# Seven half products in place of eight: the out product of blocks 1 to 8 by Strassen's scheme

## The chip, the core and the metric

The kernel runs on one core of one Trainium2 chip. The metric is the device time of one execution in microseconds (us); most executions of a kernel lie within 1% of each other. The engines are called as the profile calls them: PE is TensorE (matmuls; PEld is its weight load), DVE is VectorE, ACT is ScalarE, POOL is GpSimd, SP is the engine whose queue issues all DMA here.

## The reference

```python
# q, k, v: (8, 8, 576, 64); attention inside chunks of 64 tokens
scores = matmul(q_c, k_c.transpose(...)) / sqrt(64)
attn = softmax(scores)
x = matmul(attn, v_c)  -> tokens x 512      # 4608 x 512
a = x @ w_a                                 # 512 x 1536
b = x @ w_b
out = (a * b) @ w_out                       # 1536 x 512, float32
```

## The kernel before

The 4608 tokens are taken as 9 blocks of 512 (block 0 to 8). Each block has 12 ff tiles of 128; for each tile there are 8 matmuls of 512 columns, then ACT copies `b` out of PSUM and DVE multiplies it with `a` into `ab[ft]`. After the 12 tiles comes the out product, four groups of 128 tokens, 12 matmuls each.

```python
F = [pp.tile([128, 512], FP32, name=f"F{i}") for i in range(4)]   # a ring of four PSUM banks

def ffn_close(K, ft, us, banks):
    bT = ring("b", bsb)
    nc.scalar.copy(out=bT[:, 0:n], in_=banks[0][:, 0:n])
    nc.vector.tensor_tensor(out=ab[ft][...], in0=banks[1][:, 0:n], in1=bT[:, 0:n], op=MULT)

def out_products(tg, ft, o):
    nc.tensor.matmul(o, ab[ft][:, tg * 128:(tg + 1) * 128], wo[ft // 2][:, ft % 2, :],
                     start=(ft == 0), stop=(ft == NFT - 1))

def out_close(K, tg, o):
    t = ring("o", osb)
    nc.vector.tensor_copy(out=t, in_=o)
    # ... one or two stores to out from the SP queue
```

Attention runs in between, in units of 256 tokens. A unit goes through a chain of its own: loads of q, k, v (SP queue), casts to bf16 (GpSimd), a DMA transpose of q and k (SP queue), then the scores on PE. The order in which the program names these steps is the order in each engine's queue:

```python
for K in range(2, NBLK):
    for s in range(NFT + 4):
        step()                                   # a late normalise (DVE) or exp (ACT)
        if s < NFT: ffn(K, s)
        else:       outs(K, (s - NFT,))
        for s0, u in ((2, 2 * K + 3), (10, 2 * K + 4)):
            if s == s0 and u - 1 < NU: slot(u - 1, u if u < NU else None)  # sums, values, scores on PE
            if s == s0 + 1: cast_unit(u + 1)     # three casts on GpSimd, each waits for its DMA
            if s == s0 + 3:
                turn_unit(u + 1)                 # DMA transpose
                load_unit(u + 2)
```

Block 1 has the same parts, but its ff tiles are done in two halves of 256 tokens, because its second half's attention is not ready at first.

The softmax here doesn't subtract the row's maximum and nothing guards it: scores larger than these inputs give would overflow.

## Time and profile before

| | before |
|---|---|
| time, median | 328.55 us (3 runs, 328.37 to 329.36) |
| PE busy | 313.8 of 326.9 us |
| DVE, ACT, POOL busy | 130, 124, 76 us |
| one block, 3 to 6 | 33.1 us |
| its out product | 10.36 us: 48 matmuls of 512 columns, 216 ns each |

The profile's page gives in part 1 the busy time of each engine and its share of the span, and in part 4 the shares of the chain of work that ended last:

```profile
PE 313.8 (96%) x2698; PEld 155.4 (48%) x2698; DVE 129.9 (40%) x206; ACT 123.9 (38%) x200; POOL 76.3 (23%) x95
...
PE 80%; DMA 11%; SPq 3%; DVE 2%; ACT 2%; issue 1%; POOL 0%; DVEq 0%
```

The chain of waits of the kernel before, in order of time (start us, length us, what). L384 are the ff matmuls, L406 those of the out product, L237, L253 and L220 the attention's:

```profile
57.68 0.87 PE F L384 x8
...
116.48 10.36 PE F L406 x48
126.84 5.18 PE F L384 x24
...
132.93 13.92 PE F L384 x64
...
147.76 1.83 PE F L384 x8
149.59 10.36 PE F L406 x48
```

Two out products start 149.59 - 116.48 = 33.1 us apart, and the chain names nothing but PE in between. So in these blocks only fewer PE cycles can save time. The first line, of block 1, tells the price of a matmul of 256 columns: 0.87 us for 8, 109 ns each, half of 216.

In block 1 a second chain runs nearly as fast as PE. The timeline of the kernel before (start us, length us, engine, line, operation, tile, and in brackets the idle time before it and its releaser), for unit 5:

```profile
70.23 1.04 POOL L158 CAST qkb<-f 128x1024 bf16<-128x1024 f32 x1 [3.51 <-DMA f<-in_q_dram]
72.38 1.04 POOL L158 CAST qkb<-f 128x1024 bf16<-128x1024 f32 x1 [1.11 <-DMA f<-in_k_dram]
73.45 1.59 SPq L202 DMA_TRANSPOSE qkT<-qkb  x1
...
78.27 0.47 PE L220 MATMUL PS<-qkT 64*64 64x64 bf16 x32
```

The casts wait for DMA, the transpose for the casts, and the scores (L220) start at 78.27. A transpose takes 3.9 us in the median from issue to landing.

### The profile page before, as it was taken

What the parts mean: (1) busy time and instruction counts of PE and PEld (TensorE: products, weight loads), DVE (VectorE), ACT (ScalarE), POOL (GpSimd) and SP (SyncE); (2) the same over time, 40 slices, a digit from 0 to 9 for tenths busy, and PEclk for the clock granted to TensorE, in tenths of its full rate; (3) what the DMA queues carried; (4) which work ended last, traced back from release to release, by engine and by line L of the source; (5) the groups of instructions that cost most, each with busy time, mean ns of one, the idle gap of its engine ahead of it and who ended that gap; (6) DMA issues with size and microseconds to landing.
All of it is one profiled execution on the core that took longest, in us unless ns stands there. A gap on an engine that the chain in (4) does not pass through costs nothing.

```text
span 326.9 us, 6552 instructions
## 1 busy us (share of the span) xinstructions
PE 313.8 (96%) x2698; PEld 155.4 (48%) x2698; DVE 129.9 (40%) x206; ACT 123.9 (38%) x200; POOL 76.3 (23%) x95
## 2 busy tenths in 40 slices
PE   7599998999999999999999999999999999999995
PEld 3334444877444444444444444444444444444442
DVE  2434433444244443534253434443444353423431
ACT  3533314666326331634163416340635063303310
POOL 2556953232232231230123003210330000000000
PEclk9879999999999999999999999999999999999999
DMA  7999997999997959960996099808970600030002
GB/s 220 235 321 384 402 254 237 214 242 214 206 262 171 217 131 243 232 136 35 225 249 138 20 162 266 201 32 202 253 159 13 181 4 0 8 116 7 0 34 96
DMA packets 145693, 54.95 MB, mean 168 GB/s; under 512 B 126208, under 2 KB 139520, under 8 KB 145664
## 3 DMA queue, kind: packets, MB, share of 16 engines
q1 hardware_dynamic: 145664, 54.54, 65.6%
q8 instruction: 21, 0.34, 0.4%
q14 instruction: 8, 0.07, 0.1%
HBM read 37.75 MB, written 9.44 MB: 144 GB/s over the span
## 4 chain that ended last, share of the span: by engine, by line
PE 80%; DMA 11%; SPq 3%; DVE 2%; ACT 2%; issue 1%; POOL 0%; DVEq 0%
PE F L384 49%; PE F L406 26%; DMA wst<-in_moe_w_a_dram 5%; DMA f<-in_k_dram 3%; SPq L140 2%; PE F L237 2%; PE PS L220 2%; DMA f<-in_q_dram 1%; SPq L133 1%; PE PA L253 1%; DMA out_dram<-osb 1%; ACT inv L267 1%; DVE osb L416 1%; ACT lns L263 1%; DVE xT L272 0%
## 5 line engine op out<-in xcount | busy, mean ns | idle before, releaser
L395 ACT CAST bsb<-F 128x512 bf16<-128x512 f32 (+1 forms) x120 | 64.8, 541 | 154.1 <-PE F L384 153.9
L384 PE MATMUL F<-xT,wb 128*128 128x512 bf16 (+1 forms) x480 | 114.4, 360 | 2.6 <-DVE xT L272 1.3
L384 PE MATMUL F<-xT,wa 128*128 128x512 bf16 (+1 forms) x480 | 114.0, 359 | 1.0 <-DVE ab L396 0.4
L396 DVE TENSOR_TENSOR ab<-F,bsb 128x512 bf16<-128x512 f32 (+1 forms) x120 | 76.2, 637 | 90.7 <-PE F L384 84.6
L406 PE MATMUL F<-wo,ab 128*128 128x512 bf16 x432 | 95.4, 379 | 0.0
L384 PEld LDWEIGHTS <-wa 128*128 128x128 bf16 x480 | 46.9, 98 | 48.8 <-issue 2.1
L384 PEld LDWEIGHTS <-wb 128*128 128x128 bf16 x480 | 45.6, 98 | 47.8 <-issue 4.0
L158 POOL CAST qkb<-f 128x1024 bf16<-128x1024 f32 (+1 forms) x37 | 36.0, 973 | 134.7 <-DMA f<-in_q_dram 108.2
L406 PEld LDWEIGHTS <-ab 128*128 128x128 bf16 x432 | 42.0, 98 | 50.1
L416 DVE COPY osb<-F 128x512 f32<-128x512 f32 x36 | 24.8, 691 | 56.3 <-PE F L406 53.1
L272 DVE TENSOR_TENSOR xT<-PA,inv 128x512 bf16<-128x512 f32 x32 | 21.9, 686 | 30.1 <-ACT inv L267 30.1
L158 POOL CAST vb<-f 128x1024 bf16<-128x1024 f32 (+2 forms) x22 | 19.5, 887 | 25.8 <-DMA f<-in_v_dram 20.8
L263 ACT ACTIVATE lns<-F 128x512 f32<-128x512 f32 x32 | 17.4, 594 | 15.3 <-PE F L237 15.3
L231 ACT ACTIVATE E<-PS 128x1024 bf16<-128x1024 f32 (+1 forms) x20 | 18.8, 941 | 7.2 <-PE PS L326 4.5
L267 ACT ACTIVATE inv<-lns 128x1024 f32<-128x1024 f32 x16 | 16.9, 1057 | 0.5
L158 POOL CAST wa<-wst 128x512 bf16<-128x512 f32 x12 | 7.4, 616 | 3.2 <-DMA wst<-in_moe_w_a_dram 3.1
L158 POOL CAST wb<-wst 128x512 bf16<-128x512 f32 x12 | 7.4, 616 | 3.2 <-DMA wst<-in_moe_w_b_dram 3.0
L253 PEld LDWEIGHTS <-vb 64*64 64x64 bf16 x512 | 7.2, 109 | 1.6
L220 PE MATMUL PS<-qkT 64*64 64x64 bf16 x512 | 7.8, 202 | 0.0
L156 ACT COPY qkT<-F 128x512 bf16<-128x512 bf16 (+1 forms) x5 | 3.8, 757 | 10.2 <-PE F L180 6.9
L253 PE MATMUL PA<-E,vb 64*64 64x64 bf16 x512 | 7.2, 192 | 0.0
L158 DVE COPY qkT<-F 128x512 bf16<-128x512 bf16 x9 | 5.3, 601 | 4.6 <-PE F L303 4.2
(31 smaller groups left out, 54.7 us busy)
## 6 DMA issues: line engine op xcount, KB each, us to landing
out_dram<-osb SPq DMA_DIRECT2D x32, 256.0 KB, 2.2
f<-in_q_dram SPq DMA_DIRECT2D x28, 256.0 KB, 3.8
f<-in_k_dram SPq DMA_DIRECT2D x28, 256.0 KB, 4.3
f<-in_v_dram SPq DMA_DIRECT2D x28, 256.0 KB, 4.6
wst<-in_moe_w_out_dram SPq DMA_DIRECT2D x6, 512.0 KB, 9.2
wst<-in_moe_w_b_dram SPq DMA_DIRECT2D x5, 512.0 KB, 8.8
wst<-in_moe_w_a_dram SPq DMA_DIRECT2D x5, 512.0 KB, 8.4
f<-in_v_dram SPq DMA_DIRECT2D x16, 128.0 KB, 4.2
```

The source lines that it names most:

```text
L158: eng.tensor_copy(out=out, in_=in_)
L220: nc.tensor.matmul(o, t[j * 64:j * 64 + 64, 8 + 4 * g + m, cl * 64:cl * 64 + 64], qt, start=True, stop=True,)
L231: nc.scalar.activation(out=e[:, :, s], in_=PS[:, :, s], func=AF.Exp, scale=scale)
L253: nc.tensor.matmul(PA[j * 64:j * 64 + 64, cl, c:c + 64], vb[u % 3][cl * 64:cl * 64 + 64, g * 512 + h * 64:g * 512 + h * 64 + 64], e[cl * 6 ...
L263: nc.scalar.activation(out=lns[:, cl, :], in_=SU[cl], func=AF.Ln)
L267: nc.scalar.activation(out=inv[u % 2][:, s, :], in_=lns[:, s, :], func=AF.Exp, scale=-1.0)
L272: nc.vector.tensor_tensor(out=x.rearrange("p m (g c t) -> p c g m t", g=2, c=2)[:, cl], in0=PA[:, cl, :].rearrange(shape, g=2, m=4), in1=i ...
L384: nc.tensor.matmul(bank[:, 0:n], w[ft // 2][ft % 2][:, kt, :], x[:, kt, us[0] * 256:us[0] * 256 + n], start=(kt == 0), stop=(kt == NKT - 1),)
L395: nc.scalar.copy(out=bT[:, 0:n], in_=banks[0][:, 0:n])
L396: nc.vector.tensor_tensor(out=ab[ft][:, us[0] * 256:us[0] * 256 + n], in0=banks[1][:, 0:n], in1=bT[:, 0:n], op=MULT)
L406: nc.tensor.matmul(o, ab[ft][:, tg * 128:(tg + 1) * 128], wo[ft // 2][:, ft % 2, :], start=(ft == 0), stop=(ft == NFT - 1),)
L416: nc.vector.tensor_copy(out=t, in_=o)
```

## The change

With token halves h, ff tiles taken as pairs (f = 0 the even, 1 the odd tile), and column halves c, the out product of a block is a 2 by 2 product of matrices. Strassen's scheme does it in seven half products where the plain way needs eight, at the price of sums ahead of the products and after them. Here that is, per block, 84 matmuls of 256 columns (7 products, 6 pairs, 2 groups of 128 tokens) for 48 of 512 columns: 1/8 less PE work. The sums of `w_out` are made once, on GpSimd, in block 1; those of `ab` by DVE, three instructions for each pair; the products are put together by ACT, DVE and GpSimd.

```diff
+    def sum_wo(i, eng):                       # GpSimd, 6 pairs, once
+        b = staged["o", i].rearrange("p (x c) -> p x c", x=4)
+        y = wsum[:, i]
+        eng.tensor_tensor(out=y[:, 0:2], in0=b[:, 0:4:2], in1=b[:, 1:4:2], op=ADD)
+        eng.tensor_tensor(out=y[:, 2], in0=b[:, 1], in1=b[:, 3], op=SUB)
+        eng.tensor_tensor(out=y[:, 3], in0=b[:, 2], in1=b[:, 0], op=SUB)
+        eng.tensor_tensor(out=y[:, 4], in0=b[:, 0], in1=b[:, 3], op=ADD)
+
+    def sum_ab(i):                            # DVE, 6 pairs in every block
+        a = ab2[i].rearrange("p f (h t) -> p (f h) t", h=2)
+        y = asum[:, i]
+        nc.vector.tensor_tensor(out=y[:, 0:2], in0=a[:, 0:2], in1=a[:, 2:4], op=ADD)
+        nc.vector.tensor_tensor(out=y[:, 2:4], in0=a[:, 1:3], in1=a[:, 0:4:3], op=SUB)
+        nc.vector.tensor_tensor(out=y[:, 4], in0=a[:, 0], in1=a[:, 3], op=ADD)
+
+    def outs_fast(K, t):                      # t: which 128 tokens of each half
+        ...                                   # product(): 6 matmuls of 256 columns into the next bank of F
+        A.copy(out=m3, in_=product(of_ab(0, 0), of_wsum(2)))
+        A.copy(out=m4, in_=product(of_ab(1, 1), of_wsum(3)))
+        add(G, w, m3, m4)
+        add(V, w, product(of_asum(4), of_wsum(4)), w)
+        add(V, oa[:, HF:DM], product(of_asum(0), of_wo(1, 1)), m3)
+        add(G, y1, w, oa[:, HF:DM], SUB)
+        add(V, ob[:, 0:HF], product(of_asum(1), of_wo(0, 0)), m4)
+        add(G, y2, w, ob[:, 0:HF], SUB)
+        add(V, oa[:, 0:HF], product(of_asum(3), of_wsum(1)), y1)
+        store(K, t, oa)
+        add(V, ob[:, HF:DM], product(of_asum(2), of_wsum(0)), y2)
+        store(K, 2 + t, ob)
 ... (block 0 to block 1)
         cast_unit(3, (2,))
+        for i in range(3):
+            sum_wo(i, G)
 ... (block 1, first half)
             if ft == 3:
                 cast_unit(4)
+                for i in range(3, 6):
+                    sum_wo(i, G)
 ... (block 1, second half; the later blocks likewise)
             ffn(1, ft, (1,))
+            if ft % 2:
+                sum_ab(ft // 2)
 ...
-        for tg in range(4):
+        for t in range(2):
             step()
-            outs(1, (tg,))
+            outs_fast(1, t)
 ... (blocks 2 to 8)
-            for s in range(NFT + 4):
+            for s in range(NFT + 2):
```

The weight sums and the `ab` sums lie in the space of the weight staging buffers. The ring `osb` grows from three buffers to four.

More of the change, by code (lines that the diff above doesn't have):

```diff
@@ L27 @@
     MULT = mybir.AluOpType.mult
+    ADD = mybir.AluOpType.add
+    SUB = mybir.AluOpType.subtract
     B, H, S, D = q.shape
@@ L75 @@
     xT = [buf(f"xT_{i}", [128, NKT, BLK], BF16) for i in range(3)]
-    ab = [buf(f"ab_{i}", [128, BLK], BF16) for i in range(NFT)]
     bsb = [buf(f"bsb_{i}", [128, BLK], BF16) for i in range(3)]
-    osb = [buf(f"osb_{i}", [128, DM], FP32) for i in range(3)]
+    osb = [buf(f"osb_{i}", [128, DM], FP32) for i in range(4)]
     NP = NFT // 2
+    ab2 = [buf(f"ab_{i}", [128, 2, BLK], BF16) for i in range(NP)]
+    ab = [ab2[i // 2][:, i % 2, :] for i in range(NFT)]
     wa = [[buf(f"wa_{i}_{h}", [128, NKT, 128], BF16) for h in range(2)] for i in range(NP)]
@@ L84 @@
     NWS = 10
-    wst = [buf(f"wst_{i}", [128, 1024], FP32) for i in range(NWS)]
+    wsta = buf("wst", [128, NWS * 1024], FP32)
+    wst = [wsta[:, i * 1024:(i + 1) * 1024] for i in range(NWS)]
+    HF = DM // 2
+    wsum = wsta[:, 0:4 * 1024].bitcast(BF16)[:, 0:NP * 5 * HF]
+    wsum = wsum.rearrange("p (i n c) -> p i n c", i=NP, n=5)
+    asum = wsta[:, 4 * 1024:8 * 1024].bitcast(BF16)[:, 0:NP * 5 * HF]
+    asum = asum.rearrange("p (i n t) -> p i n t", i=NP, n=5)
+    part = buf("part", [128, 2, 5, HF], FP32)
     state = {"f": 0, "b": 0, "o": 0, "w": 0}
@@ L416, in out_close, with store @@
         nc.vector.tensor_copy(out=t, in_=o)
+        store(K, tg, t)
+    def store(K, tg, t):
         for p, n, b, s0 in runs(2 * K + tg // 2, tg % 2):
@@ L427, in outs, with product, of_ab, of_wo @@
             out_close(K, tg, o[k])
+    def sum_wo(i, eng):
[12 more added lines that the diff above has]
+    def outs_fast(K, t):
+        c = t * 128
+        m3, m4, w, y1, y2 = [part[:, t, n, :] for n in range(5)]
+        oa, ob = ring("o", osb), ring("o", osb)
+        V, A, G = nc.vector, nc.scalar, nc.gpsimd
+        def product(a, b):
+            o = nextF()[:, 0:HF]
+            for i in range(NP):
+                nc.tensor.matmul(
+                    o, a(i)[:, c:c + 128], b(i), start=(i == 0), stop=(i == NP - 1)
+                )
+            return o
+        def of_ab(f, h):
+            return lambda i: ab2[i][:, f, h * HF:(h + 1) * HF]
+        def of_wo(f, h):
+            return lambda i: wo[i][:, f, h * HF:(h + 1) * HF]
+        def of_asum(n):
+            return lambda i: asum[:, i, n]
+        def of_wsum(n):
+            return lambda i: wsum[:, i, n]
+        def add(eng, out, in0, in1, op=ADD):
+            eng.tensor_tensor(out=out, in0=in0, in1=in1, op=op)
+        A.copy(out=m3, in_=product(of_ab(0, 0), of_wsum(2)))
[10 more added lines that the diff above has]
+        store(K, 2 + t, ob)
     def fill(n):
@@ L432, in fill @@
             nc.tensor.matmul(PA[:, 0, :], zero[:, 0:128], zero, start=True, stop=True)
+    staged = {}
     with tc.manual_schedule():
@@ L450 @@
         load_half_v(0, nc.sync)
-        staged = {}
         def queue_half(i, h, ns):
@@ L670 @@
                 load_unit(7)
-        for tg in range(4):
+        for t in range(2):
             step()
-            outs(1, (tg,))
-            if tg == 1:
+            outs_fast(1, t)
+            if t == 0:
                 slot(5, 6)
                 cast_unit(7)
-            if tg == 2:
+            if t == 1:
                 turn_unit(7)
@@ L684 @@
                     ffn(K, s)
+                    if s % 2:
+                        sum_ab(s // 2)
                 else:
-                    outs(K, (s - NFT,))
+                    outs_fast(K, s - NFT)
                 for s0, u in ((2, 2 * K + 3), (10, 2 * K + 4)):
```

## The prediction

> **What bounds it now.** TensorE: busy 313.8 of 326.9 us (busy table), and the chain of waits is 80% PE. From 96 us on the slices by stage show PE fully busy: a block takes 33.1 us, of it 10.36 us out product (48 matmuls of 512 columns, 216 ns each, chain), 20.7 us ffn and about 1.9 us attention. Before 120 us there is a second chain: load, GpSimd cast, DMA transpose, next load (DMA share 0.93). In block 1 the DMA transposes of units 5 and 6 land about 0.9 and 0.2 us before their scores start (73.45 + 3.9 against 78.27; 83.72 + 3.9 against 87.7).
>
> **What the change does on PE.** 84 matmuls of 256 columns replace 48 of 512 in each of 8 blocks. 256-column matmuls already run in block 1 at 109 ns each (chain: 0.875 us for 8), with their weight loads hidden. So 9.2 us for 10.36: 1.15 us a block, 9 us in all, if nothing waits.
>
> **What it adds.**
> - DVE: 18 bf16 sums a block. Two tensor inputs in SBUF and 16-bit: the Trainium skill ("VectorE: DVE Perf Modes", perf-mode tier table) gives two elements a cycle; with the fixed 160 ns of this trace's casts that is an estimated 1.15 us per ff pair, 7 us a block. Plus ten 256-wide PSUM adds of 0.42 us for four 0.69 us copies. DVE goes from 13.5 to about 22 us of 33: not the bound in blocks 2 to 8, but in block 1's second half (256 wide) it needs 2.0 us a pair against 1.75 of PE.
> - The third half product needs the last pair's sums: about 2.4 us after the last ffn matmul, wanted at 1.8. PE waits about 0.5 us a block. The net gain of a steady block is then about 0.5 us.
> - GpSimd: 24 weight sums in block 1. No such op is in the trace; casts are 190 ns + 0.83 ns an element (1042 ns for 1024, 402 for 256). The skill ("GPSIMD Engine Reference", section 3) puts a two-input op at 2.6 cycles an element; my estimate is 0.7 us for 256 and 1.25 for 512, 3.3 us a pair, 20 us in all, in two lumps ahead of the casts of units 4 and 5. The transpose of unit 5 moves from 73.5 to about 80 us: PE waits about 5 to 6 us at its scores.
> - The block sums on GpSimd stand behind the casts of the next unit, which wait for DMA. In blocks 1 and 2 those casts end about 5 us or more after the out product starts, so DVE's first combine keeps its PSUM bank and, with 4 banks, the seventh product waits: about 4 us in block 1, 2.5 in block 2. From block 3 on the casts end about in time.
> - All four stores of a block now precede the next transpose and loads on the SP queue: 4 to 5 us later, just in time.
>
> **Sum.** Blocks 1 and 2: +12 us. Blocks 3 to 8: -3. Predicted 337.5 us, 8 in 10 between 330 and 345. Faster by over 2%: 0.05; within 2%: 0.30; slower by over 2%: 0.65.
>
> **What would show it.** Out-product matmuls at 109 ns; PE idle before scores about 78 us released by the transpose; PE idle inside the out products of blocks 1 and 2 released by a DVE add that waited for GpSimd; GpSimd adds of 0.7 us; a block of 32.5 us after block 3; a short PE wait in the third product.
>
> **What would make it wrong.** GpSimd adds near 0.83 ns an element (about 332 us); casts that come early enough; DVE sums at one element a cycle or blocked by GpSimd (later, above 340); late transposes in every block.

## The result

| | before | after |
|---|---|---|
| median | 328.96 us (4 runs) | 339.19 us (4 runs, 337.29 to 340.07) |
| ratio | | 1.0295, 95% interval 1.0237 to 1.0354: slower |
| profiled span | 326.9 us | 338.3 us |
| PE busy | 313.8 us | 309.2 us |
| DVE busy | 129.9 us | 196.0 us |
| POOL busy | 76.3 us | 131.6 us |

A ratio is the mean time of one kernel's runs over that of the other's of the same rounds, so it is not quite the ratio of the medians.

```profile
PE 309.2 (91%) x2955; PEld 184.5 (55%) x2986; DVE 196.0 (58%) x398; ACT 135.8 (40%) x232; POOL 131.6 (39%) x167
...
PE 56%; DMA 16%; SPq 8%; POOL 8%; DVE 4%; issue 4%; ACT 3%; POOLq 0%; DVEq 0%
```

These are parts 1 and 4 of the page after. PE works less, but its share of the chain fell from 80% to 56%; POOL, which had 0% of it, has 8%, and the shares of DMA and of the SP queue have grown. Where this happens is told by the times at which each block's first ff matmul starts in the PE timelines (all in us, read from the two traces; the last row is worked out):

| | block 1 | block 2 | block 3 | 4 | 5 | 6 | 7 | 8 to the end |
|---|---|---|---|---|---|---|---|---|
| before | 38.13 | 33.37 | 33.12 | 33.12 | 33.11 | 33.12 | 32.82 | 34.94 |
| after | 50.65 | 34.63 | 32.50 | 32.43 | 33.20 | 32.43 | 32.44 | 33.95 |
| difference | +12.52 | +1.26 | -0.62 | -0.69 | +0.09 | -0.69 | -0.38 | -0.99 |

Blocks 3 to 8 win 3.3 us together. Block 1 loses 12.5 us and block 2 1.3 us. The remaining 0.9 us of the 11.4 lies before block 1 (it starts at 55.17 and 56.07 us); over all runs below that start varies from 53.7 to 56.6 us with the clock that PE is granted in its first 25 us (0.72 before, 0.57 after, between 12 and 24 us). Of the change that span holds only the first few weight sums on GpSimd (from 53.02 us), and the out product of block 0 takes 14.50 us here as in the last two runs below, which have no sum there. So I compare block by block where I can.

A steady block after, in its chain of waits (L397 are ff matmuls, L475 those of the half products, L462 to L464 the three `ab` sums of a pair):

```profile
158.84 2.75 PE F L397 x12
161.59 0.40 PE F L250 x4
...
164.18 0.22 DVE xT L285
...
164.79 0.69 DVE ab L409
...
165.50 0.42 DVE wst L462
165.93 0.34 DVE wst L463
166.26 0.21 DVE wst L464
...
166.52 7.49 PE F L475 x67
```

The chain leaves PE at the end of the block's ff tiles and goes over the last `ab` product and its three sums: the third half product reads the sum that DVE makes last (L464). From the start of the out product (164.17) to the next ff matmul (173.85) it is 9.68 us.

Block 1 after, in the timeline (L453 are weight sums on GpSimd, L171 casts, L215 the transpose, L233 the scores, L493 the combining adds):

```profile
67.52 1.27 POOL L453 TENSOR_TENSOR wst<-wst 128x512 bf16<-128x512 f32 x1
...
72.76 0.95 DVE L462 TENSOR_TENSOR wst<-ab 128x512 bf16<-128x512 bf16 x1
73.64 0.94 DVE L463 TENSOR_TENSOR wst<-ab 128x512 bf16<-128x512 bf16 x1
74.50 1.34 DVE L464 TENSOR_TENSOR wst<-ab 128x256 bf16<-128x256 bf16 x1
...
76.23 0.60 PE L397 MATMUL F<-xT,wa 128*128 128x256 bf16 x4 [1.43 <-DVE ab L409]
...
77.92 2.27 POOL L171 CAST qkb<-f 128x1024 bf16<-128x1024 f32 x2
...
79.69 0.60 PE L397 MATMUL F<-xT,wa 128*128 128x256 bf16 x4 [1.55 <-DVE ab L409]
80.23 1.60 SPq L215 DMA_TRANSPOSE qkT<-qkb  x1
82.24 0.60 PE L397 MATMUL F<-xT,wa 128*128 128x256 bf16 x4 [0.65 <-DVE ab L409]
84.03 0.45 PE L233 MATMUL PS<-qkT 64*64 64x64 bf16 x32 [0.58 <-DMA qkT<-qkb]
...
101.61 1.04 POOL L171 CAST vb<-f 128x1024 bf16<-128x1024 f32 x1 [0.84 <-DMA f<-in_v_dram]
102.61 0.72 POOL L493 TENSOR_TENSOR part<-part 128x256 f32<-128x256 f32 x1
103.37 0.42 DVE L493 TENSOR_TENSOR part<-F,part 128x256 f32<-128x256 f32 x1 [5.64 <-POOL part L493]
103.84 1.17 PE L475 MATMUL F<-wst 128*128 128x256 bf16 x6 [4.45 <-DVE part L493]
...
106.72 0.58 PE L397 MATMUL F<-xT,wb 128*128 128x512 bf16 x1 [1.71 <-DVE xT L285]
```

Three things are to be seen. First, unit 5's transpose is issued at 80.23 for 73.45, because its casts stand in GpSimd's queue behind the weight sums; the scores come at 84.03 for 78.27. Second, before that PE already waits 1.43, 1.55 and 0.65 us for `ab` products of DVE, whose sums take two to five times as long here as in the steady block (L464: 1.34 us for 0.28). Third, the last cast of unit 7 waits for its load until 101.61, and the combining add of GpSimd stands behind it; DVE waits for that add, keeps its PSUM bank, and the seventh product waits 4.45 us for the bank. In the first group of the same block that wait is 1.62 us.

The windows view of the kernel after, with the busy time of each engine in us, then PE's granted clock, DMA share and GB/s, shows an after-effect of the 4.45 us:

```profile
98.00:104.00 6.00, 1.55 (x15) 1.23 (x14) 0.63 (x2) 0.00 (x0) 2.77 (x3) 1.00 0.62 176
104.00:108.00 4.00, 2.07 (x9) 1.04 (x9) 1.90 (x5) 0.00 (x0) 1.41 (x2) 0.52 0.41 137
108.00:112.00 4.00, 4.00 (x13) 1.50 (x12) 0.69 (x1) 1.91 (x3) 0.00 (x0) 0.63 0.96 217
```

The clock drops to 0.52 and 0.63 after the pause. The Trainium skill ("TensorE: Matmul & The Clock Gate", the table "Why this matters for your kernels") warns of PE-idle gaps over about 3 us; this trace agrees. The runs below put the limit somewhat lower: after the first 25 us, PE waits of 2.49, 2.83, 2.87, 3.80, 4.37 and 7.57 us were each followed by a clock near 0.50 for some us, and none of 2.18 us or less at full clock was. What this fall costs can be estimated from the lines above: 2.07 us of PE work at 0.52 and 4.00 us at 0.63 are 2.5 us more than at full clock. About 2 us of that lie in block 2, which took 34.63 us for the 32.43 of a steady block, though PE had no wait over 0.22 us in it.

### The profile page after: what moved, and what is told of

It is laid out like the page before. It is cut to its first block, busy times and chain, and to the rows that moved or that the text cites. A ratio compares the mean times of both kernels' runs of the same rounds, so it can differ in the third digit from the quotient of the medians.

```text
span 338.3 us, 7477 instructions
## 1 busy us (share of the span) xinstructions
PE 309.2 (91%) x2955; PEld 184.5 (55%) x2986; DVE 196.0 (58%) x398; ACT 135.8 (40%) x232; POOL 131.6 (39%) x167
## 4 chain that ended last, share of the span: by engine, by line
PE 56%; DMA 16%; SPq 8%; POOL 8%; DVE 4%; issue 4%; ACT 3%; POOLq 0%; DVEq 0%
PE F L397 39%; PE F L475 15%; DMA f<-in_k_dram 6%; DMA wst<-in_moe_w_a_dram 4%; DMA f<-in_v_dram 3%; SPq L123 3%; SPq L153 2%; ACT inv L280 2%; DMA f<-in_q_dram 2%; POOL qkb L171 1%; SPq L146 1%; POOL wst L453 1%; DVE ab L409 1%; PE F L250 1%; DMA qkT<-qkb 1%
## 5 line engine op out<-in xcount | busy, mean ns | idle before, releaser
L397 PE MATMUL F<-xT,wa 128*128 128x512 bf16 (+1 forms) x478 | 114.4, 361 | 4.7 <-DVE ab L409 3.8
L397 PE MATMUL F<-xT,wb 128*128 128x512 bf16 (+1 forms) x454 | 112.9, 361 | 5.4 <-DVE xT L285 3.0
L397 PEld LDWEIGHTS <-wa 128*128 128x128 bf16 x480 | 47.1, 98 | 52.3 <-issue 6.9
L397 PEld LDWEIGHTS <-wb 128*128 128x128 bf16 x480 | 46.0, 99 | 48.9 <-issue 7.3
L171 POOL CAST qkb<-f 128x1024 bf16<-128x1024 f32 (+1 forms) x37 | 36.4, 986 | 90.7 <-DMA f<-in_q_dram 64.5
L475 PEld LDWEIGHTS <-wst 128*128 128x128 bf16 x480 | 46.4, 98 | 14.8 <-issue 6.4
L475 PE MATMUL F<-wst 128*128 128x256 bf16 x288 | 38.7, 275 | 7.1 <-DVE part L493 6.1
L493 POOL TENSOR_TENSOR part<-part 128x256 f32<-128x256 f32 x16 | 11.6, 728 | 69.2 <-ACT part L496 69.2
L493 DVE TENSOR_TENSOR osb<-F,part 128x256 f32<-128x256 f32 x64 | 26.9, 423 | 11.3 <-POOL part L493 9.4
L171 POOL CAST vb<-f 128x1024 bf16<-128x1024 f32 (+2 forms) x22 | 20.1, 914 | 21.1 <-DMA f<-in_v_dram 17.0
L493 POOL TENSOR_TENSOR part<-part,osb 128x256 f32<-128x256 f32 x32 | 22.6, 728 | 14.5 <-DVE osb L493 14.5
L475 PE MATMUL F<-wst,ab 128*128 128x256 bf16 x192 | 24.7, 273 | 0.9 <-DVE ab L409 0.9
L462 DVE TENSOR_TENSOR wst<-ab 128x512 bf16<-128x512 bf16 x48 | 24.2, 504 | 1.8
L475 PE MATMUL F<-wo,wst 128*128 128x256 bf16 x192 | 23.6, 273 | 0.0
L463 DVE TENSOR_TENSOR wst<-ab 128x512 bf16<-128x512 bf16 x48 | 22.8, 474 | 0.0
L475 PEld LDWEIGHTS <-ab 128*128 128x128 bf16 x192 | 18.7, 98 | 6.2 <-DVE ab L409 1.9
L493 DVE TENSOR_TENSOR part<-F,part 128x256 f32<-128x256 f32 x16 | 6.8, 425 | 24.8 <-PE F L475 14.6
```

The source lines that it names most:

```text
L171: eng.tensor_copy(out=out, in_=in_)
L397: nc.tensor.matmul(bank[:, 0:n], w[ft // 2][ft % 2][:, kt, :], x[:, kt, us[0] * 256:us[0] * 256 + n], start=(kt == 0), stop=(kt == NKT - 1),)
L462: nc.vector.tensor_tensor(out=y[:, 0:2], in0=a[:, 0:2], in1=a[:, 2:4], op=ADD)
L463: nc.vector.tensor_tensor(out=y[:, 2:4], in0=a[:, 1:3], in1=a[:, 0:4:3], op=SUB)
L475: nc.tensor.matmul(o, a(i)[:, c:c + 128], b(i), start=(i == 0), stop=(i == NP - 1))
L493: eng.tensor_tensor(out=out, in0=in0, in1=in1, op=op)
```

## The experiments

Two theories were held against each other. **Theory Q**: the time is lost in the queue of GpSimd, where the weight sums stand ahead of casts that a transpose waits for, and the combining adds behind casts that a load is waited for. **Theory D**: it is lost on DVE, which carries 66 us more work, and whose sums PE waits for. Block lengths are read from the profiled run.

### Weight sums left out

```diff
-        for i in range(3):
-            sum_wo(i, G)
 ...
-                for i in range(3, 6):
-                    sum_wo(i, G)
 ... (block 0, before cast_pairs(2, 0, G))
+        for i in range(6):
+            V.memset(wsta[:, 640 * i:640 * (i + 1)], 0.0)
```

Expected:

> Wrong result on purpose: the 24 weight sums on GpSimd in block 1 are not done; the same store is filled with zeros by DVE in block 0, where DVE waits for DMA anyway. Theory Q (the queue of GpSimd: weight sums stand ahead of the casts of units 4 and 5, whose transposes and following loads come late): the transpose of unit 5 is issued near 74 us again instead of 80.2, and the time falls by 5 to 8 us, to 331 to 334; what stays is the wait of the out product of block 1 for the combining adds behind the casts of units 6 and 7. Theory D (the sums on DVE are what PE waits for: DVE is busy 196 us against 130): they all stay, so less than 3 us is won, 336 to 339.

Measured: 333.41 us median (330.57 to 335.03), ratio to before 1.0111 (1.0051 to 1.0171); the result is wrong. Block 1 takes 44.46 us for 50.65. The transpose of unit 5 is issued at 74.93. Of the long waits only those for the seventh product (2.87 us) and for the late normalise at the start of block 2 (2.06 us) are left:

```profile
98.14 0.81 PE L475 MATMUL F<-wst 128*128 128x256 bf16 x6 [2.87 <-DVE part L493]
101.01 0.59 PE L397 MATMUL F<-xT,wb 128*128 128x512 bf16 x1 [2.06 <-DVE xT L285]
```

So the 24 weight sums cost 6.2 us of block 1's 12.5. The zeros in their place did not make PE faster by themselves: a steady block takes 32.43 us here as in the changed kernel. Theory D's range is missed.

### Combining adds on DVE

```diff
-        V, A, G = nc.vector, nc.scalar, nc.gpsimd
+        V, A, G = nc.vector, nc.scalar, nc.vector      # in outs_fast alone
```

Expected:

> Right result: the three combining adds of each half product set go from GpSimd to DVE, the weight sums stay on GpSimd. Theory Q: the adds no longer stand behind the casts that wait for DMA; the PE waits of 1.62 and 4.45 us for the seventh product in block 1 go, and the 1.7 us at the start of block 2 with them: 332 to 335. Theory D: DVE has 48 more adds of about 0.43 us (20 us more), so the time stays or rises, 339 or more.

Measured: correct, 335.82 us median (333.92 to 337.04), ratio 1.0188 (1.0150 to 1.0227). The median is just above the range of theory Q and far from that of theory D, but the trace shows that it came about in another way than I expected. The waits for the seventh product are gone, as foretold; the one at the start of block 2, which was to go too, is still 1.49 us. Yet block 1 is only 0.8 us shorter (49.84 us), since a new wait has come in its second half. The timeline of this run:

```profile
71.36 8.68 DVE L462 TENSOR_TENSOR wst<-ab 128x512 bf16<-128x512 bf16 x1
...
78.72 1.04 POOL L171 CAST vb<-f 128x1024 bf16<-128x1024 f32 x1
...
80.96 1.01 PE L397 MATMUL F<-xT,wa 128*128 128x256 bf16 x4 [7.57 <-DVE ab L409]
```

One DVE sum, 0.42 us long elsewhere, lasted 8.68 us: from 71.36 to 80.04, until just after GpSimd's queue of weight sums and casts had run dry (79.76). PE waited 7.57 us behind it, and then ran at half clock (0.50 between 80 and 86 us), now within block 1. So weight sums cost time by holding DVE as well as by holding the casts. Block 2, with the clock at 1.00 again, is shorter by 1.36 us than after the change (33.27 us). The rest of the gain of this profiled run is its earlier start of block 1 (54.67 us).

### Both edits

Expected:

> Both edits of the two runs before, wrong result on purpose as the first of them. Theory Q: nothing of the change is left on GpSimd, blocks 1 and 2 cost about what they cost before the change plus 1 to 2 us for DVE in the second half of block 1, and the six later blocks win 0.6 us each: 325 to 328. Theory D: 336 or more.

Measured: 328.37 us median (326.53 to 331.20), ratio 0.9975 (0.9911 to 1.0039), wrong result as intended: the same time as before the change. Block 1 takes 40.93 us and block 2 32.55. DVE does all of its sums and 48 adds more than in the changed kernel, and the loss is gone; no wait in blocks 1 and 2 is over 1.88 us, and the clock does not fall after them. This refutes theory D as the main cause: DVE's own load does not make the loss. What is left of block 1's loss, 2.8 us, is what DVE does cost: waits of 0.2 to 0.8 us for `ab` in the second half, and 1.88 us for the late normalise. The median came out a little above my range; I had counted 1 to 2 us for those.

### Writes in place of the weight sums

Two parts of the loss in block 1 could each be the cause: late casts, or DVE sums slowed beside GpSimd's. The Trainium skill ("SBUF — State Buffer", section "Who interferes with whom") says that a DVE instruction with two SBUF inputs contends with a GpSimd instruction that reads SBUF, not with one that only writes it. So this run gives GpSimd writes alone, about as long:

```diff
-        eng.tensor_tensor(out=y[:, 0:2], ...)      # and the three other sums
+        t = wsta[:, 640 * i:640 * (i + 1)]
+        for n in (640,) * 5:
+            eng.memset(t[:, 0:n], 0.0)
```

Expected:

> Wrong result on purpose: in place of the four weight sums of a pair GpSimd does five writes of 640 zeros, about as long (3.2 us for 3.5), which read nothing. It tells two parts of the loss in block 1 apart. In the changed kernel the bf16 sums on DVE take 0.95, 0.94 and 1.34 us while GpSimd sums run beside them, against 0.42, 0.42 and 0.28 later, and PE waits 3.6 us for ab there. If the slowed DVE sums cost the time by themselves, the time falls by 3 to 4 us, to 335 to 336. If the order in the queue of GpSimd does (theory Q), DVE sums take 0.42 us and the waits for ab go, but PE waits as much longer for the transpose of unit 5 (issued at 80 us): within 1.5 us of the changed kernel, 337.5 to 340.5.

Measured: 338.18 us median (337.73 to 339.50), ratio 1.0261 (1.0243 to 1.0278), wrong result. In its timeline (L460 and L461 are the second and third sum of a pair, L233 the scores):

```profile
75.21 0.42 DVE L460 TENSOR_TENSOR wst<-ab 128x512 bf16<-128x512 bf16 x1
75.54 0.28 DVE L461 TENSOR_TENSOR wst<-ab 128x256 bf16<-128x256 bf16 x1
...
83.65 0.65 PE L233 MATMUL PS<-qkT 64*64 64x64 bf16 x32 [4.37 <-DMA qkT<-qkb]
```

Beside writes the sums run at full speed (0.42 and 0.28 us), as the page says, and PE no longer waits for `ab`. It waits 4.37 us for the transpose instead, which is issued at 79.78 us. In the changed kernel the waits for `ab` and for the transpose up to these scores add up to 4.21 us (1.43 + 1.55 + 0.65 + 0.58). So there the slowed DVE sums filled a wait that the late transpose would have made anyway. The time alone would show less. It is that of the changed kernel to within about 1 us, but block 1 is 1.5 us shorter (49.17 us) and block 2 1.0 us longer (35.66), and the clock falls twice here instead of once: the undivided wait is followed by 0.50 between 82 and 88 us, while the four short waits of the changed kernel left it at 1.00. By an estimate, the 4.35 us of PE work at 0.50 cost 2.2 us; without them the time would lie near 336 us, the other theory's value. So the waits decide here, and that the time fell in the range of theory Q is partly luck.

### Half products from block 3 on

Nothing of this kind needs to stand in block 1. Here blocks 1 and 2 keep the plain out product, and GpSimd does the weight sums in block 2, behind the casts of units 8 and 9.

```diff
+                        if K == 2:                       # after cast_unit(u + 1)
+                            for i in range(3):
+                                sum_wo(i + (3 if s0 == 10 else 0), G)
 ...
+                elif K == 2:
+                    outs(K, (s - NFT,))
```

Expected:

> Right result: blocks 1 and 2 keep the plain out product, the weight sums stand on GpSimd in block 2 behind the casts of units 8 and 9, and the half products are used in blocks 3 to 8 alone. Theory Q: blocks 1 and 2 cost what they did before the change, since nothing new stands ahead of casts that a transpose waits for soon; the six blocks win 0.6 us each: 3 to 4 us under the kernel before, 324 to 326, ratio about 0.989. If the loss of the change were spread over all its blocks, this would not be faster than before.

Measured: correct, 331.26 us median of 6 (327.25 to 332.02), ratio 1.0029 (0.9975 to 1.0083). This is a miss: no gain. Blocks 1 and 2 are as before the change (38.35 and 33.12 us), as foretold, but block 3 takes 37.11 us. Its timeline:

```profile
130.47 4.35 DVE L462 TENSOR_TENSOR wst<-ab 128x512 bf16<-128x512 bf16 x1
...
133.51 1.04 POOL L171 CAST vb<-f 128x1024 bf16<-128x1024 f32 x1
...
136.01 1.08 PE L397 MATMUL F<-xT,wa 128*128 128x512 bf16 x4 [2.83 <-DVE ab L409]
```

GpSimd was still busy with the second lot of weight sums and the casts behind it when block 3's first `ab` sum came. The sum lasted from 130.47 to 134.82, again until GpSimd's queue was empty (134.55), and PE waited 2.83 us. After that the clock was 0.61 between 136 and 140 us, so block 3 lost 4.7 us against a steady block (32.43), more than the wait. The edit had moved the collision, not taken it away.

### The wanted sum first

```diff
+        nc.vector.tensor_tensor(out=y[:, 4], in0=a[:, 0], in1=a[:, 3], op=ADD)
         nc.vector.tensor_tensor(out=y[:, 0:2], ...)
         nc.vector.tensor_tensor(out=y[:, 2:4], ...)
-        nc.vector.tensor_tensor(out=y[:, 4], in0=a[:, 0], in1=a[:, 3], op=ADD)
```

Expected:

> As e4_from_block_3, and the three sums of a pair on DVE in another order: first the one that the third product reads. In the changed kernel PE waits 0.5 us in each block, in the third product (a block's out product takes 9.7 us where 84 matmuls at 109 ns make 9.2). If that wait is the sum's, each of six blocks wins 0.4 to 0.5 us more: 2.5 to 3 us under e4_from_block_3, 321.5 to 323.5, ratio about 0.981. If it is another's, nothing changes.

Measured: correct, 326.18 us median (325.62 to 329.58), ratio 0.9934 (0.9877 to 0.9990). The steady block goes from 32.43 to 32.09 us, and its out product from 9.68 to 9.33. So the wait in the third product was the sum's. It is worth 0.35 us a block, a little under the 0.4 to 0.5 that I expected. The time is above my range because the collision in block 3 is still there (a wait of 2.18 us). It is 5.1 us under the run before, more than I expected: in the profiled runs block 3 takes 34.43 us for 37.11, since after this shorter wait the clock stayed at 1.00. That part is no merit of the edit that I could show.

### The transpose after two stores

```diff
+                    if s == NFT + 1:
+                        turn_unit(2 * K + 5)
+                        load_unit(2 * K + 6)
                     outs_fast(K, s - NFT)
 ...
-                    if s == s0 + 3:
+                    if s == s0 + 3 and (K == 2 or s0 == 2):
                         turn_unit(u + 1)
```

Expected:

> As e6_wanted_sum_first, and the next unit's transpose and loads are issued after the first two stores of a block, not after all four. In the changed kernel the transpose was late once (block 6: PE waits 0.6 us before the scores). If late transposes cost more than that, this wins 1 us or more; by my reading it wins 0 to 0.7 us: 321 to 323.

Measured: correct, 328.27 us median of 6, but three of the six runs are over 1.5% above its fastest and count as slow; the ratio of the fast ones is 0.9871 (0.9813 to 0.9928). That ratio leans on this split, so I don't read a gain from it. The trace shows what the edit does: block 5, which in the run before took 32.86 us for one late transpose, takes 32.09 us like the others. (The expectation calls it block 6; counted from 0 as here, the wait is in block 5, at 212.85 us in the changed kernel.) The worth is 0.8 us, once. The wait in block 3 is there as before (2.49 us), and here it was followed by a clock of 0.57 between 136 and 140 us: block 3 takes 36.43 us for 34.43.

### Weight sums on DVE

```diff
-                        if K == 2:
-                            for i in range(3):
-                                sum_wo(i + (3 if s0 == 10 else 0), G)
 ... (sum_wo takes parts now; after ffn(K, s))
+                    if K == 2:                          # two of the 24 after each ff tile
+                        sum_wo(s // 2, V, (0, 1) if s % 2 == 0 else (2, 3))
```

Expected:

> As e7_transpose_early, and the weight sums leave GpSimd: DVE does them in block 2, two of the 24 after each ff tile, where its trace shows 1.03 us idle between two products. In the three runs from block 3 on PE waited 2.2 to 2.8 us at the start of block 3 for an ab product, while GpSimd still did weight sums and a DVE sum with two inputs stood still beside them. If GpSimd's sums hold those of DVE up, the wait goes: 2 to 3 us under e7_transpose_early, profiled span 321 to 323, ratio to before 0.975 to 0.983. If that wait has another cause, or if DVE's added sums delay block 2 as much, nothing is won.

Measured: correct, 323.69 us median (320.84 to 324.99), ratio 0.9805 (0.9757 to 0.9854). From 90 us on, PE waits only once for another engine (0.28 us for `ab`, in block 8), and its chain of waits shows steady blocks of 32.09 us (L480 are the half products):

```profile
179.97 9.33 PE F L480 x84
...
212.06 9.33 PE F L480 x84
...
244.15 9.33 PE F L480 x84
```

Block 2 takes 33.12 us although DVE makes all weight sums in it, and block 3 32.08 us. The wait at the start of block 3 was GpSimd's doing. The profiled span is 319.2 us, under my range of 321 to 323: block 3 wins 4.3 us, the wait of 2.49 us and the lower clock after it. This kernel beats both, clear of noise; whether it beats the kernel before by 2% is not decided by the interval.

### No sums on GpSimd

```diff
-        V, A, G = nc.vector, nc.scalar, nc.gpsimd
+        V, A, G = nc.vector, nc.scalar, nc.vector      # in outs_fast, on top of the kernel above
```

Expected:

> As e8_weight_sums_on_dve, with the three combining adds on DVE too, so GpSimd has only the casts of before. If GpSimd's adds cost nothing once the casts are done in time (theory Q), the six blocks stay at 32.1 us each and only the last store comes 0.3 to 0.5 us earlier: within 1 us of e8_weight_sums_on_dve. If the queue of GpSimd still costs in later blocks, 2 us or more are won; if DVE is near its limit, it gets slower.

Measured: correct, 322.95 us median (321.55 to 324.49), ratio 0.9785 (0.9747 to 0.9823). That is within 1 us of the kernel above, and the blocks are the same to 0.06 us, apart from 0.2 us in block 2 (33.35 us). The combining adds on GpSimd cost nothing where the casts ahead of them are done in time. In block 1 of the changed kernel they were not.

## Why the prediction was right

The time (339.19 us for 337.5, range 330 to 345) and the direction were right, and the mechanism was in the main the one named: weight sums ahead of casts in GpSimd's queue, and combining adds behind casts. That the sum came so close was partly luck, as the last points show. Point by point:

- **PE work.** I expected 84 matmuls of 109 ns, 9.2 us. Undisturbed they take 9.33 us, 111 ns each. Right.
- **The wait in the third product**, 0.5 us expected. It costs 0.35 us of a block, shown by the order of the sums. Right.
- **A steady block** of 32.5 us: 32.43 to 32.50. Right. One late transpose (block 5) costs another 0.8 us.
- **GpSimd's sums** of 0.7 and 1.25 us: 0.73 and 1.30 us, 21.3 us in all for 20 expected. The estimate from the skill's page on GpSimd was right, and the transpose of unit 5 came at 80.2 us, as estimated.
- **The wait at unit 5's scores**, 5 to 6 us expected. There it is only 0.58 us; 3.6 us of it were spent before, for `ab` products of DVE that were slowed beside GpSimd's sums. The run with writes alone turns one into the other (4.37 us at the scores). I had named the slowing only as a risk that would come on top. It does not come on top; it fills the same gap.
- **Combining adds behind casts**: about 4 us in block 1 and 2.5 in block 2 expected. In block 1 it was 1.62 + 4.45 us, more. In block 2 it was nothing: GpSimd's last cast ended at 132.0 us, 0.4 us after the out product began at 131.67, and the add was on time. The term of block 2 failed. Before the change that cast ended 4.9 us after the start of the out product (121.17 against 116.31 us); after it the out product starts 15.4 us later and the cast only 10.9 us later, so the casts had caught up.
- **What I had not foreseen**: 1.71 us at the start of block 2 for a normalise that stands on DVE behind the last combining adds, and the lower clock after the 4.45 us pause, an estimated 2.5 us.
- **The sum**: blocks 1 and 2 cost 13.8 us for 12 expected, blocks 3 to 8 win 3.3 us for 3 expected. Errors in single terms cancelled: the 2.5 us for combining adds in block 2 did not come, and the lower clock, which is in no term, cost about as much. That is luck.

What stays open is what decides whether a DVE sum takes turns with GpSimd (about 1 us each in the changed kernel) or is held until GpSimd's queue is empty (8.68 and 4.35 us in two runs, 3.56 and 3.87 us in the two built on the second of them), what sets the clock in the first 25 us, and how much of the scatter between runs of one kernel the falls of the clock make.

## What to carry to other kernels

An engine that is 23% busy is not free: what counts is what stands in its queue behind the new work, and who waits for that. Put one-time work where the queue behind it has slack, and don't put a step that the critical engine waits for behind one that waits for DMA. Where DVE has idle time between its instructions, as it had here, give it sums in portions that fit that time before GpSimd gets them in one lump. And look at the clock after a long wait of PE: here waits of 2.49 us and more cost more than their own length.

## What the Trainium skill lacked or had wrong

- "SBUF — State Buffer": it says that the loser of the port shared by DVE and GpSimd is blocked for the other's whole instruction. It does not say that the hold can outlast one instruction. Two runs here show a DVE sum held through a row of GpSimd instructions until that queue ran dry: 8.68 us and 4.35 us for a sum of 0.42 us.
- "TensorE: Matmul & The Clock Gate", section "Back-to-back issue gap": about 131 ns for a sustained pair of weight load and matmul of 512 columns. Here it is 216 ns (10.36 us for 48), and for 256 columns 109 ns in the ff tiles and 111 ns in the half products; the page's formula for an isolated matmul gives 216 and 109.
- "GPSIMD Engine Reference", section 3: 2.6 cycles an element for two inputs holds (2.1 to 2.2 ns an element between 256 and 512), but the page gives no fixed time for short sums; here 256 elements take 0.73 us, so about 0.17 us of it is fixed.
- "VectorE: DVE Perf Modes": two elements a cycle for 16-bit sums holds (0.42 us for 512, 0.28 for 256). The cycle table's fixed 58 cycles do not: the two times give about 0.14 us, some 135 cycles at the page's 0.96 GHz. The page says as much below its table (about 150 cycles for a copy), so this bears out its text and only the table is wrong.
